# A block-sort attention with an FFT mixer: Sinkhorn on 128 partitions, K and Q of batch 0 ahead of V, variances on ScalarE, add and clamp in one instruction

## The chip, the cores and the metric

The kernel runs on one core of a Trainium2 chip. The time is the device time of one execution in microseconds; the median of three runs before the change is 257.31 us. TensorE is called PE below (PEld are its weight loads), VectorE DVE, ScalarE ACT, GpSimd POOL and SyncE SP.

## The reference

Two stages follow one another: an attention in which the blocks of K and V are first mixed by a matrix P that Sinkhorn's iteration makes, and a Fourier mixer with a feed-forward network. Shortened:

```python
# q, k, v: (4 batches, 8 heads, 768 positions, 64)   sort_net: (4, 8, 8, 8)
P = sort_net
for _ in range(5):
    P = np.exp(P - P.max(-1, keepdims=True))
    P = P / P.sum(-1, keepdims=True)              # rows
    P = P / P.sum(-2, keepdims=True)              # columns
k_s = einsum('bhij,bhjcd->bhicd', P, k in 8 blocks of 96 positions)
v_s = einsum('bhij,bhjcd->bhicd', P, v in 8 blocks of 96 positions)
attn = softmax(q_block @ k_s_block.T / 8)         # in each block, 96 x 96
x = (attn @ v_s) with the heads side by side      # (4, 768, 512)

u = x + real(fft(fft(x, axis=1), axis=2))
un = (u - mean(u)) / sqrt(var(u) + 1e-6)          # over the last axis
out = u + relu(un @ w_ch1) @ w_ch2                # 512 -> 2048 -> 512
```

## The kernel before, in words

The whole work is one list of operations (`P.add`), each with a function that issues its instructions and with the buffers it reads and writes. The order on each engine is not found by the planner: the table `ORDER` gives for each of the five engines the numbers of its operations, and `schedule` only merges the five lists, gives out the pool buffers and works out planned times. These times serve one purpose in the program that is issued: in planned gaps of PE, `spins` puts dummy products (L1973) that read `pack` and write an unused bank, until batch 0's first Fourier results are planned to be done. An instruction waits on the chip only for the semaphores of its data and its buffer.

`tmpk` and `hk` are keys of the buffer `hr`, which holds the feed-forward activations late in the program and, at the start, V of batches 0 and 1 (`hr_72`) and the small tiles of Sinkhorn (`hr_73`).

The work by stages:

- Loads. SP issues the small ones (`pw` from `sort_net`, the constants `pack`, and rows), POOL the large ones: the two halves of V of batches 0 and 1 (`load_v`, 1.5 MB of fp32 each), then the first halves of K and Q of batch 0, then POOL's own memsets, then the second halves of K and Q.
- Sinkhorn (L761 to L776). The 32 matrices (4 batches by 8 heads) stand on 32 partitions, 64 numbers each. Five rounds, each one exponential on ACT and six small DVE instructions. PE then transposes the result, DVE forms `zhi`, `ztm` and `zlo` (L789 to L795), PE spreads `zhi` over partitions, and DVE makes from it `bdk`, the block matrix for K (L805, two halves of the heads), and, in `bdv_make` (L985), the block matrices `bdv16` and `bdv32` for V. ACT keeps a copy, `tkh` (L814), for the later batches.
- V of batches 0 and 1. `v_path` sums V over the positions of a block on PE (psm, L873), copies V in eight parts to `vcx` in the order that the mixing needs (L855 and the `vcp` operations, on ACT and DVE), and `v_mean` and `v_mix` (L945) multiply by `bdv16`; the result goes to `vsf` (L855).
- Attention of a batch, four pairs of heads: `kqt` mixes K (L1140, and L1170 in batch 0) and transposes Q (L1205), `scores` makes the scores (L1236) and ACT their exponentials (L1245), `av` multiplies with V (L1275) and DVE divides into `rt` (L1292).
- Fourier mixer: `dft1` (L1349 and others) along positions, `dft2` (L1427 to L1496) along channels. `dft2` runs for six tiles of 128 positions in each batch. DVE adds x and the transform (L1453 for the first three tiles), then takes the variance with `bn_stats` and `bn_aggr` (L1494, L1496), except for the three tiles of batch 0's first half (`split`), where the sum comes with the addition and DVE scales it (L1483) and ACT takes the squares (L1488).
- Feed-forward. Batches 0 and 1 use `ff1` (L1558) and `mlp` (L1615). Batches 2 and 3 (`SEVEN`) use `ff1_seven` and `ff2_chunk`, a scheme with seven products for eight. There DVE adds a bank and a copy of another (`add`, L1702) and then clamps at zero (`relu`, L1708), in 48 tiles of 128 x 384.

## Time and profile before

| | |
|---|---|
| runs before, us | 257.59, 256.82, 257.31; median 257.31 |
| span of the profiled execution, us | 254.8 (the page lists no time of this execution beside the span) |
| PE busy | 245.2 us, 96% of the span, 2996 products |
| DVE busy | 234.2 us, 92%, 597 instructions |
| ACT busy | 165.3 us, 65%, 376 instructions |
| POOL busy | 57.5 us, 23%, 88 instructions |
| read from and written to memory | 29.07 MB, 6.29 MB; 139 GB/s over the span |
| chain that ended last, by engine | PE 71%, issue 9%, DVE 9%, ACT 8%, POOL 2% |

The profile is of one execution and counts from its first instruction; the span ends with its last. "Busy" is the time in which an engine carried out instructions, its dummy products among them. The chain that ended last is followed back from the last instruction, at each step to what released it. In the prediction's rows a timeline row gives start, length, engine, line, operation, and in brackets the idle time before it with what ended it.

### The profile page before, as it was taken

To read this page: it belongs to the slowest core of one execution; us is meant where nothing else is said; L and a number is where in the kernel's file an instruction comes from. 1 tells how busy PE (TensorE), PEld (TensorE's weight loads), DVE (VectorE), ACT (ScalarE), POOL (GpSimd) and SP (SyncE) were. 2 spreads that over 40 slices of the span, in tenths; PEclk is the share of its full clock that TensorE was granted. 3 is DMA by queue.
4 is the path that set the end of the run, shared out by engine and by line. 5 is a ranking of instruction groups with operands and counts; after the bars stand their busy time and mean duration, and the time that the engine had idled before them with its cause. 6 is when DMAs were issued, how large, how long until landed. Compare 5 with 4: busy or idle time off the path is not lost.

```text
span 254.8 us, 7461 instructions
## 1 busy us (share of the span) xinstructions
PE 245.2 (96%) x2996; PEld 167.0 (66%) x2996; DVE 234.2 (92%) x597; ACT 165.3 (65%) x376; POOL 57.5 (23%) x88
## 2 busy tenths in 40 slices
PE   4999999999999999999999999999999999999992
PEld 1347875566566676644667757888657887567882
DVE  4799998999999989978999998999999999999993
ACT  2599998999968879956797377622687323773000
POOL 8974532234400770003100000210100000050013
PEclk9999999999999999999999999999999999999998
DMA  6999999999942699524132002530202400220025
GB/s 134 202 215 300 210 217 214 208 211 187 150 49 75 86 193 120 64 43 136 44 38 44 1 8 46 98 125 35 82 3 41 84 3 0 85 88 37 3 82 207
DMA packets 42809, 26.54 MB, mean 104 GB/s; under 512 B 30234, under 2 KB 39208, under 8 KB 42772
## 3 DMA queue, kind: packets, MB, share of 16 engines
q0 software_dynamic: 23664, 18.35, 42.9%
q1 hardware_dynamic: 19110, 7.71, 15.0%
q8 instruction: 23, 0.38, 0.6%
q14 instruction: 12, 0.10, 0.1%
HBM read 29.07 MB, written 6.29 MB: 139 GB/s over the span
## 4 chain that ended last, share of the span: by engine, by line
PE 71%; issue 9%; DVE 9%; ACT 8%; POOL 2%; DMA 1%; POOLq 0%; DVEq 0%
PE bank L1558 15%; PE bank L1794 14%; PE bank L1694 12%; PE bank L1615 9%; PE bank L1275 4%; PE bank L1440 3%; PE bank L945 2%; PE bank L1236 2%; ACT vcx L855 2%; PE bank L1349 2%; POOL out_dram L1593 2%; DVE rt L1292 1%; PE bank L1444 1%; PE bank L1047 1%; PE bank L1140 1%
## 5 line engine op out<-in xcount | busy, mean ns | idle before, releaser
L1558 PE MATMUL bank<-ut,w1sb 128*128 128x384 f16 x256 | 48.2, 326 | 0.0
L1714 ACT COPY vsf<-bank 128x384 f32<-128x384 f32 x48 | 21.6, 482 | 24.0 <-PE bank L1694 23.6
L1245 ACT ACTIVATE ex<-bank 96x384 f32<-96x384 f32 x64 | 29.3, 487 | 7.6 <-PE bank L1236 6.2
L1558 PEld LDWEIGHTS <-w1sb 128*128 128x128 f16 x256 | 23.1, 98 | 14.1 <-issue 0.3
L1570 ACT ACTIVATE hr<-bank 128x384 f16<-128x384 f32 x56 | 26.3, 491 | 8.5 <-PE bank L1558 8.5
L1593 POOL DMA_INDIRECT out_dram<-u,rows x9 | 9.4, 1042 | 97.4 <-DVE u L1811 72.5
L1794 PEld LDWEIGHTS <-hr 128*128 128x128 f16 x288 | 28.2, 98 | 4.6
L1702 DVE TENSOR_TENSOR hr<-bank,vsf 128x384 f16<-128x384 f32 x48 | 25.2, 548 | 1.6 <-PE bank L1694 1.0
L1615 PE MATMUL bank<-w2sb,hr 128*128 128x512 f16 x96 | 23.6, 380 | 0.0
L1794 PEld LDWEIGHTS <-vcx 128*128 128x128 f16 x216 | 21.1, 98 | 3.2
L1694 PE MATMUL bank<-ut,w1sb 128*128 128x384 f16 x96 | 20.7, 326 | 0.0
L1794 PE MATMUL bank<-w2sb,hr 128*128 128x256 f16 x144 | 18.7, 272 | 0.0
L1275 PEld LDWEIGHTS <-eb 97*128 97x128 f16 x416 | 15.7, 98 | 3.1 <-issue 0.4
L1794 PE MATMUL bank<-kq,vcx 128*128 128x256 f16 x144 | 17.5, 272 | 0.0
L1694 PEld LDWEIGHTS <-w1sb 128*128 128x128 f16 x128 | 12.5, 98 | 7.5
L612 POOL DMA_DIRECT2D kq<-in_q_dram x18 | 15.4, 866 | 8.8 <-PE bank L1558 4.2
L1292 DVE TENSOR_TENSOR rt<-bank,rz 128x384 f16<-128x384 f32 x32 | 16.9, 547 | 0.2
L1275 PE MATMUL bank<-vsf,eb 97*128 97x65 f16 x416 | 16.9, 193 | 0.0
L855 ACT CAST ks<-bank 128x384 f16<-128x384 f32 x27 | 14.4, 555 | 3.1 <-PE bank L1140 3.0
L1260 ACT ACTIVATE eb<-ex,negone 96x384 f16<-96x384 f32 x26 | 15.9, 616 | 0.1
L855 ACT CAST vsf<-bank 96x512 f16<-96x512 f32 x22 | 14.2, 679 | 1.4 <-PE bank L945 1.4
L1258 DVE TENSOR_SCALAR eb<-ex 96x384 f16<-96x384 f32 x38 | 13.9, 371 | 0.6 <-ACT ex L1245 0.4
(195 smaller groups left out, 535.5 us busy)
## 6 DMA issues: line engine op xcount, KB each, us to landing
w1sb<-in_moe_w_ch_dram POOLq DMA_DIRECT2D x4, 512.0 KB, 18.6
w2sb<-in_moe_w_ch_dram POOLq DMA_DIRECT2D x4, 512.0 KB, 21.5
hr<-in_v_dram POOLq DMA_DIRECT2D x2, 768.0 KB, 8.8
kq<-in_v_dram POOLq DMA_DIRECT2D x2, 768.0 KB, 12.7
kq<-in_k_dram POOLq DMA_DIRECT2D x8, 192.0 KB, 6.5
kq<-in_q_dram POOLq DMA_DIRECT2D x16, 96.0 KB, 6.7
out_dram<-u SPq DMA_DIRECT2D x5, 256.0 KB
kq<-in_k_dram POOLq DMA_DIRECT2D x2, 384.0 KB, 11.7
```

What stands on the lines that cost most here:

```text
L855: (nc.scalar.copy if e == "ACT" else V.tensor_copy)(dst, src)
L1245: nc.scalar.activation(ex.ap[0:96], pss[h2].ap[0:96, 0:384], AF.Exp, scale=SCALE),
L1260: nc.scalar.activation(ed, src, AF.Identity, bias=negone[0:96])
L1275: nc.tensor.matmul(po.ap[:, 65 * T:65 * T + 65], eb.ap[:, e0:e0 + 128], vsf[0:97, vi:vi + 65], start=(n == 0), stop=(n == len(WIN[T]) - 1) ...
L1292: P.add({"DVE": (0.465, 0.56)}, lambda _: V.tensor_tensor(rt.ap[:, :, D * h:D * h + D], po3()[:, :, 0:D], rz.ap[:, :, None].broadcast_to([ ...
L1558: nc.tensor.matmul(ps.ap[:, 0:GT], w1sb[:, c, 128 * fc:128 * fc + 128], ut.ap[:, c, :], start=(c == 0), stop=(c == 3))
L1570: nc.scalar.activation(hr[g][:, fc, :], ps.ap[:, 0:GT], AF.Relu)
L1615: nc.tensor.matmul(ps.ap, hr[g][:, fc, 128 * tt:128 * tt + 128], w2sb[:, fc, :], start=(fc == 0), stop=(fc == 15))
L1694: nc.tensor.matmul(ps.ap[:, 0:GT], lhs[:, c, fi], rhs()[:, c, :], start=(start and c == 0), stop=(c == 1), skip_group_check=True)
L1702: return P.add({"DVE": (0.47, 0.57)}, lambda _: V.tensor_tensor(hr[g][:, fc, :], p.ap[:, 0:GT], o.ap, op=ALU.add), r=r, w=hk(g, fc, fc + 1 ...
L1714: P.add({"ACT": act(GT)}, lambda _: nc.scalar.copy(x.ap, A.ap[:, 0:GT]), r=[A], w=[x], prio=pr_v - 1, tag="pc", after=avs)
L1794: nc.tensor.matmul(ps.ap[:, o:o + 256], lhs()[:, fc], rhs[:, fc], start=(start and fc == 0), stop=(fc == 7), skip_group_check=True)
```

## The change

**Sinkhorn.** The 256 rows of the 32 matrices now stand on 128 partitions in two halves (batches 0 and 1, and 2 and 3), eight numbers on each partition. The first row sum comes with the exponential. A matrix `skc` of constants holds a block matrix of ones, `ones8`: its product with the 128 x 8 tile sums over the eight rows of a matrix and leaves the sum on each of its partitions. The column sums are a DVE accumulation on the same instruction as the multiplication. The first normalization spreads the tile into a block matrix (`spread`) and multiplies it with a selector on PE, which transposes the blocks. Four rounds follow, each with an exponential on ACT, a product on PE and three DVE instructions, for each half. At the end `bdv16` and `bdv32` are made from the tile itself with a mask (L804), `bdk` from one product of `bdv16` of half 0 (L816, L822); `zhi`, `ztm`, `zlo`, `pt` and the function `bdv_make` go.

**Later batches.** `tkh` is no longer a copy on ACT at the start: `make_tk8` makes it by two products from `bdv16` of both halves.

**Loads.** K and Q of batch 0 (first halves) are issued ahead of V's halves; `x0`, `skc` and `x1` ahead of `pack`. The four loads of `w2` keep their places in POOL's order.

**Variances.** `split` holds for all tiles: every variance is taken with the sum that comes with the addition and an ACT square; in tiles 3 to 5 the sum has two parts, added in the scaling.

**Add and clamp.** In `ff1_seven` one custom DVE instruction, `TENSOR_ADD_SAT`, adds and limits to 0 and the largest float.

**Order.** `ORDER` is replaced as a whole, on all engines. Copies of V wait in the program for Sinkhorn operations other than before (`after=`).

```diff
 ORDER = { "PE": (
-        "77 69 78 73 79 91 139 123 125 127 92 97 129 211 141 143 0 103 218 "
+        "0 39 69 43 73 48 78 53 83 88 58 94 97 137 153 141 155 139 157 98 "
...
-    for n, nm in enumerate(("pw", "pack", "vrow", "erow", "rrow",
-                            "rows")):
+    for n, nm in enumerate(("x0", "skc", "x1", "pack", "vrow", "erow",
+                            "rrow", "rows")):
         load_c(nm, -5000.0 + n, "SP")
-    load_v(0, 0, -5000.0)
-    load_v(0, 1, -4999.0)
-    load_qk("k", 0, 0, -4998.0)
-    load_qk("q", 0, 0, -4997.0)
+    load_v(0, 0, -4998.0)
+    load_v(0, 1, -4997.0)
+    load_qk("k", 0, 0, -5000.0)
+    load_qk("q", 0, 0, -4999.0)
...
+        own3 = own[:, :, None].broadcast_to([128, 16, NB])
+        step(d, lambda _: V.tensor_reduce(mx, x, axis=AX.X, op=ALU.max),
+        step(d, lambda _: V.tensor_scalar(z, x, mx, None, op0=ALU.subtract),
+        step({"ACT": (0.3, 0.32)}, lambda _: nc.scalar.activation(
+            E, z, AF.Exp, accum_out=r))
+        step(d, lambda _: V.reciprocal(ri, r))
+        step({"DVE": (0.26, 0.27)}, lambda _: V.scalar_tensor_tensor(
+            spread[t].rearrange("p (g j) -> p g j", j=NB),
+            E[:, None, :].broadcast_to([128, 16, NB]), ri, own3,
+            op0=ALU.mult, op1=ALU.mult), ["skc"])
+        ps = Buf("pf")
+        step(m_, lambda _: nc.tensor.matmul(ps.ap[:, 0:8], spread[t], seli),
+        step(d, lambda _: V.tensor_reduce(
+            cs_, ps.ap[:, 0:8], axis=AX.X, op=ALU.add), [ps])
+        step(d, lambda _: V.reciprocal(ci, cs_))
+        for it in range(4):
+                nc.scalar.activation(E, ps.ap[:, 0:8] if it == 0 else F,
+                                     AF.Exp, scale=ci)
+            step(m_, lambda _, pr=pr: nc.tensor.matmul(
+                pr.ap[:, 0:8], ones8, E), ["skc"], [pr])
+            step(d, lambda _, pr=pr: V.reciprocal(RI, pr.ap[:, 0:8]), [pr])
+            step(d, lambda _: V.scalar_tensor_tensor(
+                F, E, 1.0, RI, op0=ALU.mult, op1=ALU.mult, accum_out=cs_))
+            step(d, lambda _: V.reciprocal(ci, cs_))
+        for n, d_ in enumerate((bdv16[t], bdv32[t])):
+            P.add({"DVE": (0.22, 0.29)}, lambda _, d_=d_:
+                  V.scalar_tensor_tensor(
+                      d_, F[:, None, :].broadcast_to([128, 16, NB]), ci,
+                      own3, op0=ALU.mult, op1=ALU.mult),
...
+        bk.ap[:, 0:64], repk, bdv16[0].rearrange("p g i -> p (g i)")[
+            :, 0:64]), r=[("bdv16", 0), "pack"], w=[bk], tag="psk")
...
-              after=sks[-1:] if b == 0 else [])
+              r=[pt], w=[(qt, 0), (qt, 1)], tag="qtev")
...
-        split = (b, g) == (0, 0)
+        split = True
...
-                return P.add({"DVE": (0.47, 0.57)}, lambda _: V.tensor_tensor(
-                    hr[g][:, fc, :], p.ap[:, 0:GT], o.ap,
-                    op=ALU.add), r=r, w=hk(g, fc, fc + 1), prio=pr_v,
-                    tag="fadd")
-
-            def relu(g, fc):
-                P.add({"DVE": (0.16, 0.24)}, lambda _: V.tensor_scalar(
-                    hr[g][:, fc, :], hr[g][:, fc, :], 0.0, None, op0=ALU.max),
+                return P.add({"DVE": (0.47, 0.57)}, lambda _: V._custom_dve(
+                    TENSOR_ADD_SAT, out=hr[g][:, fc, :], in0=p.ap[:, 0:GT],
+                    in1=o.ap, s0=FMAX, s1=0.0), r=r,
+                    w=hk(g, fc, fc + 1), prio=pr_v, tag="fadd")
```

The changed order, at three places as the instructions stand in the two programs. First the start of ACT, from its table load to batch 0's first exponentials of scores (L1245 before, L1223 after; `vcx` is the copy of V, `ks` and `qt` are K mixed and Q transposed); before:

```order
L711 ACT_TABLE_LOAD
L766 ACTIVATE hr_73<-hr_73 32x64 x5
L855 COPY vcx<-hr_72 128x96x8 x4
L855 CAST ks_77<-bank_64 128x3x8x16
L888 ACTIVATE vb<-vsum 128x128
L855 CAST ks_78<-bank_65 128x3x8x16
L855 CAST ks_78<-bank_61 128x3x8x16
L855 COPY qt_79<-bank_64 128x768
L855 CAST mean_117<-bank_65 128x128
L814 CAST tkh<-bank_62 128x256
L1245 ACTIVATE ex_82<-bank_64 96x384
```

and after:

```order
L777 ACT_TABLE_LOAD
L777 ACTIVATE hr_73<-hr_73 128x8 x2
L792 ACTIVATE hr_73<-bank_61,hr_73 128x8
L792 ACTIVATE hr_73<-bank_62,hr_73 128x8
L792 ACTIVATE hr_73<-hr_73 128x8 x6
L714 ACT_TABLE_LOAD
L863 COPY vcx<-hr_72 128x96x8 x2
L863 CAST ks_78<-bank_63 128x3x8x16
L863 COPY qt_79<-bank_64 128x768
L863 CAST ks_78<-bank_65 128x3x8x16
L863 CAST ks_77<-bank_62 128x3x8x16
L863 COPY vcx<-hr_72 128x96x8
```

Two copies of V instead of four stand ahead of the copies of `ks` and `qt`, the third follows them, the copy to `tkh` is gone, and a second table load stands between Sinkhorn's last exponential and V. Next ACT at its first evacuations of mixed V (`vsf` from a bank of L945 before, of L953 after), with exponentials of scores (`ex`) and other copies about them; before:

```order
L855 CAST vsf<-bank_68 96x64x8
L1245 ACTIVATE ex_82<-bank_63 96x384
L855 CAST vsf<-bank_66 96x64x8
L1245 ACTIVATE ex_84<-bank_63 96x384
L1245 ACTIVATE ex_82<-bank_65 96x384
L855 CAST vsf<-bank_68 96x64x8
L855 COPY rv<-rr 64x255
L855 CAST hi_92<-bank_64 128x257
L855 CAST ks_78<-bank_61 128x3x8x16
L855 COPY rv<-rr 64x256
```

and after:

```order
L863 COPY qt_81<-bank_64 128x768
L863 CAST ks_78<-bank_63 128x3x8x16
L863 COPY un_100<-bank_61 64x4x32
L1223 ACTIVATE ex_83<-bank_62 96x384
L863 CAST vsf<-bank_68 96x64x8
L863 CAST vsf<-bank_63 96x64x8
L863 CAST vsf<-bank_64 96x64x8
L863 CAST vsf<-bank_62 96x64x8
L863 CAST vsf<-bank_65 96x64x8
L863 CAST vsf<-bank_63 96x64x8
L863 CAST ex_83<-bank_64 64x512
L863 COPY qt_79<-bank_61 128x768
```

Three of the copies to `vsf` stood between exponentials of scores; now six follow one another. Last, the end of Sinkhorn on DVE, down to the second copy of V (`bank_61` and `bank_62` in the L805 and L822 rows are the spread matrix for K); before:

```order
L775 RECIPROCAL hr_73<-hr_73 32x8
L776 TENSOR_TENSOR hr_73<-hr_73 32x64
L855 COPY vcx<-hr_72 128x96x8
L789 TENSOR_TENSOR hr_73<-bank_61,pack 64x256
L855 COPY vcx<-hr_72 128x96x8
L805 TENSOR_TENSOR bdk<-bank_62,pack 128x512 x2
L880 TENSOR_REDUCE vsum<-bank_66 128x64
```

and after:

```order
L799 SCALAR_TENSOR_TENSOR hr_73<-hr_73 128x8
L798 RECIPROCAL hr_73<-bank_65 128x8
L799 SCALAR_TENSOR_TENSOR hr_73<-hr_73 128x8
L801 RECIPROCAL hr_73<-hr_73 128x1
L804 SCALAR_TENSOR_TENSOR bdv_0_112<-hr_73 128x128
L863 COPY vcx<-hr_72 128x96x8
L822 TENSOR_TENSOR bdk<-bank_61,pack 128x512
L804 SCALAR_TENSOR_TENSOR bdv_0_111<-hr_73 128x128
L822 TENSOR_TENSOR bdk<-bank_61,pack 128x512
L801 RECIPROCAL hr_73<-hr_73 128x1
L804 SCALAR_TENSOR_TENSOR bdv_1_113<-hr_73 128x128
L863 COPY vcx<-hr_72 128x96x8
```

`bdk` is now made from `bdv16` of half 0 (L804, 128 x 128), with one copy of V ahead of it, instead of from `zhi` (L789); the second half's last reciprocal and `bdv16` come behind `bdk`.

204 lines of the change are left out of this document (81 added, 123 removed), and 199 rows, old and new, of the table ORDER.

## The prediction

> **What bounds the kernel now.** I read the busy time by stage first, then the chain of waits, then the first 30 us instruction by instruction. Busy time by stage (columns: stretch, its length, then busy us and in brackets the instructions of PE, PEld, DVE, ACT and POOL, PE's granted clock, DMA share and GB/s):
>
> ```profile
> 0.00:14.90 14.90, 10.58 (x40) 4.05 (x40) 9.95 (x39) 7.33 (x10) 13.84 (x23) 1.00 0.95 173
> 14.90:43.00 28.10, 27.48 (x540) 19.53 (x540) 27.27 (x73) 26.21 (x61) 11.30 (x18) 1.00 1.17 234
> 43.00:59.00 16.00, 16.00 (x306) 9.83 (x303) 14.30 (x44) 15.30 (x41) 4.54 (x6) 1.00 1.17 210
> 59.00:150.00 91.00, 90.89 (x1350) 57.62 (x1339) 85.51 (x191) 69.67 (x162) 17.55 (x25) 1.00 0.68 83
> 150.00:246.00 96.00, 96.00 (x745) 72.43 (x744) 92.75 (x243) 46.77 (x106) 7.12 (x12) 1.00 0.18 51
> ```
>
> From 59 to 246 us TensorE has work in 186.9 of 187 us. Before that two other engines are full: in 14.9 to 43, VectorE (DVE) 27.2 and ScalarE (ACT) 26.2 of 28.1 us; in 43 to 59, ACT 15.3 and DVE 14.3 of 16. The chain of waits says which of them counts. Its pieces in order of time (start, length, what):
>
> ```profile
> 10.12 5.66 ACT vcx L855 x4
> ...
> 58.53 0.38 ACT hr L1570
> 59.24 1.09 PE bank L1037 x8
> ```
>
> Up to 59 us the chain is mostly ACT and DVE pieces, beginning with the copies of V; from 59.2 us nearly every piece is a matmul. So a microsecond saved on DVE is worth something only ahead of 59 us, and after that the end moves with the time at which TensorE became full. The start, row by row (start, length, engine, line, what; in brackets the idle time before and who ended it):
>
> ```profile
> 1.27 1.32 POOL L612 DMA_DIRECT2D hr<-in_v_dram  x2 [0.82 <-POOLq L1990]
> 2.33 0.21 DVE L761 TENSOR_REDUCE hr<-hr 32x8 f32<-32x64 f32 x1 [1.46 <-DMA hr<-in_sort_net_dram]
> 3.71 4.46 PE L1973 MATMUL bank<-pack 128*128 128x480 f16 x12 [3.71 <-DMA pack<-k_pack]
> 8.66 1.46 PE L873 MATMUL bank<-hr,pack 128*128 128x512 f16 x6 [0.49 <-DMA hr<-in_v_dram]
> 9.95 1.58 PE L1973 MATMUL bank<-pack 128*128 128x480 f16 x7
> 10.03 5.76 ACT L855 COPY vcx<-hr 128x768 f16<-128x768 f16 x4
> 11.39 0.21 DVE L776 TENSOR_TENSOR hr<-hr 32x64 f32<-32x64 f32 x1
> 11.53 0.80 DVE L855 COPY vcx<-hr 128x768 f16<-128x768 f16 x1
> 13.56 1.29 DVE L805 TENSOR_TENSOR bdk<-bank,pack 128x512 f16<-128x512 f32 x2 [0.17 <-PE bank L799]
> 14.93 0.53 PE L1170 MATMUL bank<-bdk,kq 128*64 128x128 f16 x12
> 16.42 0.36 PEld L1205 LDWEIGHTS <-kq 128*64 128x64 f16 x12 [0.21 <-DMA kq<-in_q_dram]
> 18.29 0.49 PE L999 MATMUL bank<-bdv,vb 128*128 128x128 f32 x2
> 19.33 0.41 PE L945 MATMUL bank<-bdv,vcx 128*128 128x64 f16 x8
> ```
> ```profile
> 24.11 0.69 ACT L855 CAST vsf<-bank 96x512 f16<-96x512 f32 x1
> 28.04 0.57 PE L1275 MATMUL bank<-vsf,eb 97*128 97x65 f16 x13
> 250.30 0.42 DVE L1811 TENSOR_TENSOR u<-bank,u 128x256 f32<-128x256 f32 x1 [0.34 <-PE bank L1794]
> ```
>
> Sinkhorn runs from 2.33 to 11.60 us; L789 to L805 turn its result into the block matrix `bdk`; the first product of batch 0 (L1170) starts at 14.93, the first `v_mix` (L945) at 19.33, the first attention product (L1275) at 28.04. TensorE fills its waits with dummy products (L1973). The loads of V behind this (size, us from issue to landing):
>
> ```profile
> hr<-in_v_dram POOLq DMA_DIRECT2D x2, 768.0 KB, 8.8
> ```
>
> The first half of V landed at 8.6 (L873 waited for it) and the second at about 12.2: the mean over both is 8.8, so 17.6 together; the first took 8.6 - 1.27 = 7.3, which leaves 10.3 from the second issue at some 1.9. K and Q of batch 0, of one size, follow in the queue; Q ends L1205's wait at 16.4. So a V half took 3.6 us, K and Q some 2.0 each, and all four were in by 16.2 to 16.4.
>
> **The change part by part.** The unit costs (count, then busy us and mean ns of one):
>
> ```profile
> L770 DVE RECIPROCAL hr<-hr 32x8 f32<-32x8 f32 x5 | 1.0, 191 | 0.2
> L711 ACT ACT_TABLE_LOAD x1 | 1.3, 1283 | 0.7 <-PEq L1990 0.7
> L766 ACT ACTIVATE hr<-hr 32x64 f32<-32x64 f32 x5 | 1.3, 255 | 6.8 <-DVE hr L776 6.0 <-DVE hr L763 0.8
> L789 DVE TENSOR_TENSOR hr<-bank,pack 64x256 f16<-64x256 f32 x1 | 0.4, 403 | 0.0
> L814 ACT CAST tkh<-bank 128x256 f16<-128x256 f32 x1 | 0.4, 381 | 0.0
> L855 ACT CAST ks<-bank 128x384 f16<-128x384 f32 x27 | 14.4, 555 | 3.1 <-PE bank L1140 3.0
> L1494 DVE BATCH_NORM_STATS2 st<-u 128x6 f32<-128x512 f32 x15 | 10.2, 682 | 0.1
> L1496 DVE BATCH_NORM_AGGREGATE mv<-st 128x2 f32<-128x6 f32 x21 | 3.1, 167 | 0.0
> L1483 DVE TENSOR_SCALAR mv<-mv 128x1 f32<-128x1 f32 x3 | 0.5, 153 | 0.1
> L1453 DVE DVE_READ_ACCUMULATOR u<-rt,bank 128x1 f32 x3 | 0.2, 83 | 0.0
> L1488 ACT ACTIVATE ex<-u,mv 128x512 f16<-128x512 f32 x3 | 2.2, 722 | 0.0
> L1488 ACT ACTIVATION_READ_ACCUMULATOR ex<-u,mv 128x1 f32 x3 | 0.6, 186 | 0.0
> L1702 DVE TENSOR_TENSOR hr<-bank,vsf 128x384 f16<-128x384 f32 x48 | 25.2, 548 | 1.6 <-PE bank L1694 1.0 <-ACT vsf L1714 0.3
> L1708 DVE TENSOR_SCALAR hr<-hr 128x384 f16<-128x384 f16 x48 | 10.3, 250 | 0.1
> ```
>
> *Loads.* With K and Q first, V's halves come third and fourth: 16.2 - 3.6 = 12.5 us and 16.2 us, each 3.9 later than now. ACT, which starts copying V at 10.03 (1.44 us a copy), can start at 12.5. K and Q are there by about 9, which nobody needs so early.
>
> *Sinkhorn.* `pack` is now fourth on SP's queue instead of second. From the first small load's landing (2.33) to `pack`'s (3.71) are 1.4 us, an upper bound for one issue; I take 0.45 each, so the dummies start at 3.7 + 0.9 = 4.6, and two of them at 0.4 us stand ahead of the first Sinkhorn product: 5.4. Its operand is ready about 4.5 (2.33, then two maxima and two subtractions, an exponential, reciprocals and the spread tile, nine small steps of about 0.24). Such a product has no row; L999, also fp32 with 128 weight columns, takes 0.49 for 128 columns, so for 8 columns between 0.25 and 0.5; I take 0.4. Sum and reciprocal then cost 2 x 0.19 and two handovers, and `ci` of half 0 stands at 6.2. One round is an exponential (0.26 at most), a product (0.4), three small DVE instructions (0.19), and five gaps of 0.05: 1.48 us. (Today five rounds take 9.27 us with the start, 1.85 each, of which one exponential and six DVE instructions of 0.2 are 1.46: 0.39 for seven gaps.) Four rounds end at 12.1. But the table for TensorE puts half 1's last product and five dummies ahead of half 0's last, which waits for the other half's exponential: +0.9, 13.0. The masked matrix `bdv16`, 0.3 beside the 0.40 of L789, makes it 13.3. Today the same point, `zhi` behind the copy that ends at 12.33, is 12.7. So Sinkhorn saves no time by itself (bounds: 12.4 without the cross wait, 14.9 if the products run as slowly as the dummies do at first).
>
> *To the first product.* On DVE a copy of V (0.80) stands ahead of `bdk`, and its data have been in since 12.5: 13.3 + 0.8 + half of 1.29 = 14.75. On TensorE seven dummies (7 x 0.22) and the six V sums (1.46) stand ahead of the first product: from 12.7 on 1.5 + 1.5, so 15.7 at the latest, 14.9 if the dummies were done earlier. I take 15.0 for the first product, as now.
>
> *From there to attention.* V's second half at 16.2, three plus three V sums around scores that wait for ACT (two copies to 15.4, then four evacuations of `ks` and `qt` at 0.55 to 17.6), reduction 0.7, mean and its masked form about 1.9: the first `v_mix` at about 21.5 instead of 19.33. The table for TensorE puts more of batch 0 ahead of it: all 48 K products of batch 0, 36 Q transposes and 32 score products, where now 24, 24 and 8 are. So the eight `v_mix` follow one another, and ACT takes six of their evacuations in a row: 21.5 + 0.5 + 6 x 0.69 = 26.2 for the first attention product, against 28.04: 1.85 us earlier. That is the term that carries the forecast.
>
> *Variances.* In batch 0's second half three DVE statistics (0.68 + 0.17 each) go and three scalings (0.15) and six accumulator reads (0.08) come: -1.6 us on DVE. ACT gains three squares at 0.72 + 0.19: +2.7. The two engines have 0.7 + 1.7 = 2.4 us free in 43 to 59, and the sum rises by 1.1, so most of it fits; I charge 0.35, between 0 (copies move to DVE in the new tables) and 1.35 (half of 2.7). For the other 18 tiles, after 59 us, DVE loses 18 x 0.85 = 15 us and regains about 5, beside a full TensorE: 0.
>
> *Add and clamp.* 48 clamps (0.25 each) go from batches 2 and 3. The fused instruction has no row; its bounds are the add, 0.55, and add plus clamp, 0.80, and I take 0.55 since it reads the same two fp32 operands. All of it lies beside a full TensorE: 0 either way, since even 0.80 is today's sum. *Tail:* the same last product, addition (250.30) and store: 0. *Second table load on ACT:* the first one, at the very start, ends ahead of the data; the second takes 1.28 us. Its last exponential ends at 11.2 without the cross wait and at about 12.05 with it (13.0 less a product, two DVE steps and gaps), so ACT is ready for V at 12.5 or at 13.3, where V lands at 12.5. Half of such a delay would be lost, since DVE does not share it: 0 to 0.4, and I charge 0.2.
>
> The Trainium skill, "ScalarE: Activation LUTs", What ACT_TABLE_LOAD costs, gives about 1.38 us of drain behind each load, 2.66 in all. By that the copies of V would start 1.4 later, and half of that would be lost: a gain of 0.6 instead of 1.3. No row of the trace can tell: after the only load ACT waited for data.
>
> **Sum.** -1.85 + 0.35 + 0.2 = -1.3 us on a span of 254.8: 253.5. The page lists no time of the profiled execution beside its span; the three runs' median, 257.31, lies 2.5 us above the span, and I keep that: **256.0 us**.
>
> **Rivals.** *VectorE was the hidden bound* (faster still). In 150 to 246 DVE is busy 92.8 of 96 us; if matmuls wait briefly for it, the 22 us or so taken off DVE (15 - 5 for the variances, 12 for the clamps) would show. For: 97%. Against: TensorE's row is 96.00 of 96. A tenth of 22 us recovered gives 253.8.
>
> *Cold TensorE* (no change). In the start the first dummies come every 0.4 us (12 in 4.46 us), after 9.95 every 0.2. Both clocks read 1.00 in the stage rows, so this is not the granted clock. After the change the first dummies are spread between waits, and if the fast pace comes only after some 4 us without a break, the five and the seven dummies in Sinkhorn's end run at 0.4: +1.0 and +1.4 less 0.5 of slack, and `bdk` comes 1.9 later: 257.9. For: 12 dummies in a row needed 4 us. Against: 5 + 7 may be enough. The Trainium skill, "TensorE: Matmul & The Clock Gate", Part 1, states this rule: half rate until about 3.4 us of sustained work; the 4 us of slow dummies agree with it.
>
> *ACT and DVE start too late* (slower). The chain up to 59 us runs on these two, and both stand idle longer: ACT begins at 12.5 instead of 10.03 (+2.5), DVE is free of Sinkhorn at 13.3 instead of 11.6 (+1.7). Work taken from them there: `zhi` and its two companions 1.2, `tkh` 0.4. (4.2 - 1.6) / 2 = +1.3: 258.6. For: both are over 93% busy from 14.9 to 43. Against: the work done first is now what the chain needs first. It decides once the first attention product comes later than 28.0.
>
> **How the numbers follow.** Forecast 0.50, hidden bound 0.17, cold TensorE 0.12, late start 0.21. The runs before spread over 0.77 us, so 0.3% (0.8 us) is about what a measurement tells from no change. Faster: 0.50 + 0.17 = 0.67; same: 0.12, less 0.01 of it; slower: 0.21 + 0.01 = 0.22. Low end: the hidden bound's 253.8 with the cross wait (0.8) and the table's share (0.2) gone, 252.8. High end: the late start, 258.6, and 0.3 for its spread, 258.9.
>
> **What would show it.** Right: V's first copy on ACT between 12.5 and 13.3, first product near 15, first `v_mix` near 21.5, first attention product near 26.2, TensorE full from about 57.5, the fused instruction at 0.55. Wrong: the first attention product after 28, dummies at 0.4 us behind 10 us, or waits of TensorE between 59 and 246 that shrink.

## The result, and the profile after

The changed kernel takes 269.4 us (median of four runs, 268.43 to 269.66) against 257.09 before: a ratio of 1.047, 95% interval 1.045 to 1.050. The forecast was 256.0, with a range up to 258.9. The profiled span is 267.9 us, 13.1 more than before; time less span is 1.8 us in this execution (269.66), not the 2.5 that the forecast carried over. Medians below leave out runs more than 1.5% above the fastest of their kernel: two of four with the other form of L775 alone, one of four in the fourth corner. Busy time by stage, with the edges and columns of the prediction's first table:

```profile
0.00:14.90 14.90, 3.28 (x12) 1.98 (x12) 10.29 (x13) 2.31 (x7) 13.84 (x24) 1.00 0.91 171
14.90:43.00 28.10, 27.05 (x349) 17.73 (x350) 23.27 (x81) 22.26 (x44) 8.17 (x14) 1.00 0.86 163
43.00:59.00 16.00, 15.42 (x332) 10.39 (x330) 15.24 (x46) 14.92 (x36) 4.07 (x6) 1.00 1.06 211
59.00:150.00 91.00, 90.22 (x1448) 57.19 (x1446) 83.39 (x218) 68.70 (x167) 20.93 (x29) 1.00 0.90 105
150.00:246.00 96.00, 96.00 (x736) 70.11 (x733) 88.05 (x220) 54.88 (x133) 6.64 (x12) 1.00 0.16 46
```

In the first 14.9 us ACT has done 2.3 us of work instead of 7.3 and TensorE 12 products instead of 40; from 59 to 246 us TensorE has work in 186.2 of 187 us, where it was 186.9. The loss lies in the start. Its rows (start, length, engine, line, what, idle time before):

```profile
3.13 0.16 DVE L773 TENSOR_REDUCE hr<-hr 128x1 f32<-128x8 f32 x1 [0.49 <-DMA hr<-in_sort_net_dram]
3.21 8.24 DVE L775 TENSOR_SCALAR hr<-hr 128x8 f32<-128x8 f32 x2
4.07 5.84 POOL L700 MEMSET eb<- 96x1672 f16 x4
6.90 0.98 PE L1953 MATMUL bank<-pack 128*128 128x480 f16 x2 [6.90 <-DMA pack<-k_pack]
10.57 0.45 POOL L712 MEMSET negone<- 128x1 f32 x1
11.47 0.21 ACT L777 ACTIVATE hr<-hr 128x8 f32<-128x8 f32 x1 [9.45 <-DVE hr L775]
```
```profile
19.88 1.28 ACT L714 ACT_TABLE_LOAD   x1
21.18 2.90 ACT L863 COPY vcx<-hr 128x768 f16<-128x768 f16 x2
21.25 2.68 PE L1953 MATMUL bank<-pack 128*128 128x480 f16 x7
22.09 0.35 DVE L804 SCALAR_TENSOR_TENSOR bdv<-hr 128x128 f16<-128x128 f32 x1
25.19 0.53 PE L1149 MATMUL bank<-bdk,kq 128*64 128x128 f16 x12
32.53 0.41 PE L953 MATMUL bank<-bdv,vcx 128*128 128x64 f16 x8
```
```profile
38.65 0.97 PE L1253 MATMUL bank<-vsf,eb 97*128 97x65 f16 x26
```

Both maxima are there at 3.3 us, and the two subtractions behind them (L775, eight numbers on each partition) end at 11.45: ACT gets its first exponential after 9.45 us of waiting. In those 8.2 us POOL issues the loads of V and then carries out its memsets (4.07 to 11.02) without a pause. No semaphore shows this wait: the row counts it as the instruction's own time, and 8.24 of DVE's 10.29 busy us in the first stage are this standing still. So an instruction here does not wait for the semaphores of its data and its buffer alone. Everything behind is late by that and more: `bdv16` of half 0 ends at 22.44 (13.3 forecast), the first product of K comes at 25.19 (15.0), the first `v_mix` at 32.53 (21.5), the first attention product at 38.65 (26.2; 28.04 before).

### The profile page after: what moved, and what is told of

Same layout as the page of the kernel before. It is cut to its first block, busy times and chain, and to the rows that moved or that the text cites. A ratio compares the mean times of both kernels' runs of the same rounds, so it can differ in the third digit from the quotient of the medians.

```text
span 267.9 us, 7506 instructions
## 1 busy us (share of the span) xinstructions
PE 247.8 (92%) x3006; PEld 171.2 (64%) x3006; DVE 235.5 (88%) x607; ACT 165.0 (62%) x388; POOL 57.3 (21%) x88
## 4 chain that ended last, share of the span: by engine, by line
PE 73%; issue 10%; DVE 6%; ACT 5%; POOL 2%; DMA 1%; POOLq 0%; SPq 0%; DVEq 0%; ACTq 0%
PE bank L1547 16%; PE bank L1775 13%; PE bank L1683 9%; PE bank L1604 8%; PE bank L1253 4%; DVE hr L775 3%; PE bank L1418 3%; PE bank L1327 3%; PE bank L1214 2%; PE bank L1953 2%; POOL out_dram L1582 2%; ACT ex L1223 2%; PE bank L953 2%; PE bank L881 1%; PE bank L1422 1%
## 5 line engine op out<-in xcount | busy, mean ns | idle before, releaser
L1547 PEld LDWEIGHTS <-w1sb 128*128 128x128 f16 x256 | 23.4, 98 | 14.9 <-issue 0.4
L1582 POOL DMA_INDIRECT out_dram<-u,rows x9 | 10.2, 1137 | 105.7 <-DVE u L1792 73.5
L1223 ACT ACTIVATE ex<-bank 96x384 f32<-96x384 f32 x64 | 29.0, 489 | 3.7 <-PE bank L1214 2.4
L1691 DVE CUSTOM_DVE_ANT_0 hr<-bank,vsf 128x384 f16<-128x384 f32 x48 | 25.1, 552 | 5.4 <-PE bank L1683 4.6
L1559 ACT ACTIVATE hr<-bank 128x384 f16<-128x384 f32 x44 | 20.8, 488 | 7.3 <-PE bank L1547 7.2
L1775 PEld LDWEIGHTS <-vcx 128*128 128x128 f16 x216 | 21.1, 98 | 3.3
L863 ACT CAST vsf<-bank 96x512 f16<-96x512 f32 x21 | 13.6, 684 | 9.8 <-PE bank L953 9.7
L1775 PE MATMUL bank<-w2sb,hr 128*128 128x256 f16 x144 | 18.0, 273 | 0.0
L1253 PE MATMUL bank<-vsf,eb 97*128 97x65 f16 x416 | 17.5, 193 | 0.5 <-issue 0.4
L1236 DVE TENSOR_SCALAR eb<-ex 96x384 f16<-96x384 f32 x48 | 16.5, 357 | 0.9 <-ACT ex L1223 0.9
L1683 PEld LDWEIGHTS <-w1sb 128*128 128x128 f16 x128 | 12.5, 98 | 7.4
L1953 PE MATMUL bank<-pack 128*128 128x480 f16 x26 | 10.4, 503 | 6.9 <-DMA pack<-k_pack 6.9
L1683 PE MATMUL bank<-qt,kq 128*128 128x384 f16 x64 | 14.8, 326 | 0.0
## 6 DMA issues: line engine op xcount, KB each, us to landing
w2sb<-in_moe_w_ch_dram POOLq DMA_DIRECT2D x4, 512.0 KB, 21.9
out_dram<-u SPq DMA_DIRECT2D x5, 256.0 KB
```

The costliest lines, as they stand in the source:

```text
L1223: nc.scalar.activation(ex.ap[0:96], pss[h2].ap[0:96, 0:384], AF.Exp, scale=SCALE),
L1236: V.tensor_scalar(ed, src, -1.0, None, op0=ALU.add)
L1253: nc.tensor.matmul(po.ap[:, 65 * T:65 * T + 65], eb.ap[:, e0:e0 + 128], vsf[0:97, vi:vi + 65], start=(n == 0), stop=(n == len(WIN[T]) - 1) ...
L1547: nc.tensor.matmul(ps.ap[:, 0:GT], w1sb[:, c, 128 * fc:128 * fc + 128], ut.ap[:, c, :], start=(c == 0), stop=(c == 3))
L1559: nc.scalar.activation(hr[g][:, fc, :], ps.ap[:, 0:GT], AF.Relu)
L1683: nc.tensor.matmul(ps.ap[:, 0:GT], lhs[:, c, fi], rhs()[:, c, :], start=(start and c == 0), stop=(c == 1), skip_group_check=True)
```

## The experiments

### Is it the form of one instruction, against POOL?

Three kernels. In the first the subtraction takes another form; in the second the old kernel gets one small instruction of the suspected form; in the third POOL's long memsets go to DVE, ahead of its first data.

```diff
-        step(d, lambda _: V.tensor_scalar(z, x, mx, None, op0=ALU.subtract),
+        step(d, lambda _: V.tensor_tensor(
+            z, x, mx.broadcast_to([128, NB]), op=ALU.subtract),
```

> The changed kernel, with only the subtraction of the maximum (L775) in another form: a TENSOR_TENSOR with the maximum broadcast over the eight numbers, the form that the kernel before uses at L763, instead of a TENSOR_SCALAR with the maximum as scalar. Theory POOL: the two TENSOR_SCALARs (8.2 us each, both done at 11.45) stand still because POOL carries out memsets from 4.07 to 11.0 us. Then the subtractions take about 0.2 us each, the first exponential starts near 3.6 instead of 11.47, everything up to the first product of batch 0 moves up by some 7.9 us, and the time is about 261.5 us (between 260.5 and 262.5). Theory DATA: they wait for a load or for ACT; then the form changes nothing: 269.4 us. About 4.4 us over the kernel before stay in either case, from something else.

```diff
 # the kernel before
                 V.tensor_tensor(pw, pw, rmax ..., op=ALU.subtract)
+                V.tensor_scalar(rs, rmax, rmax[:, 0:1], None, op0=ALU.subtract)
```

> The kernel before with one more DVE instruction: behind the subtraction of L763 a TENSOR_SCALAR from SBUF to SBUF, 32 x 8 fp32, whose result nothing reads. Theory POOL: it stands until POOL's memsets end at 11.0 us, so Sinkhorn ends some 7.5 to 8 us later and the time is 263 to 266 us. Theory DATA, or a small instruction's own price: +0.2 us, 257.3 us.

```diff
-        P.add({"POOL": (1.5, 1.6)}, lambda _, n=n: nc.gpsimd.memset(
+        P.add({"DVE": (0.45, 0.5)}, lambda _, n=n: nc.vector.memset(
             eb4[0:96, n, :], 0.0), w=[("ebz", n)], ...)
```

> The changed kernel with the four memsets of eb (5.84 us of POOL's 7) on DVE at the very start, where DVE waits for its first data until 2.48; L775 keeps its form. Theory POOL: the memsets that stay on POOL then run from 4.07 to about 5.3, and the subtractions end there, or at the end of the DMA issues behind them if these count too (about 6), instead of at 11.45: 263 to 264.5 us. Theory DATA: 269.4 us. The four memsets on DVE themselves: 0.5 us each, ended before 2.5, nothing.

Timeline rows of the three, in this order:

```profile
3.07 0.28 DVE L775 TENSOR_TENSOR hr<-hr 128x8 f32<-128x8 f32 x2
7.02 0.98 PE L1954 MATMUL bank<-pack 128*128 128x480 f16 x2 [7.02 <-DMA pack<-k_pack]
8.27 0.17 DVE L788 TENSOR_REDUCE hr<-bank 128x1 f32<-128x8 f32 x1 [3.44 <-PE bank L786]
20.51 0.53 PE L1150 MATMUL bank<-bdk,kq 128*64 128x128 f16 x12
```
```profile
2.69 8.28 DVE L767 TENSOR_SCALAR hr<-hr 32x8 f32<-32x8 f32 x1
10.85 0.16 POOL L705 MEMSET pmt<- 128x6 f16 x1
```
```profile
4.43 1.29 DVE L776 TENSOR_SCALAR hr<-hr 128x8 f32<-128x8 f32 x2
4.80 0.49 POOL L709 MEMSET pmt<- 128x6 f16 x1
```

Theory POOL holds in all three. With the other form both subtractions take 0.28 us in the same place. One TENSOR_SCALAR whose result nobody reads, put into the kernel before, takes 8.28 us there, until POOL's last memset ends (11.01), and costs 10.5 us (267.24 against 256.78; ratio 1.040, 1.038 to 1.042). With four memsets off POOL the pair takes 1.29 us and ends at 5.72, 0.43 after the last memset, as in the changed kernel (11.45 and 11.02). The Trainium skill, "SBUF — State Buffer", SBUF: two separate sides, states a rule of this kind: DVE and POOL share a pair of ports; of a DVE operation in a two-port mode and a POOL operation the one that starts first holds the pair for the whole instruction, and a DVE operation with two SBUF inputs is shut out only by a POOL operation that reads SBUF. The three runs agree with it in which form waits (a memset reads nothing); beyond it, the wait here goes on through a whole row of POOL instructions, nine memsets and the DMA issues ahead of them. Whether the issues alone would hold DVE stays open: in the second kernel the instruction begun at 2.69 was not done when the memsets began at 4.04, and POOL had only issued loads until then; but in the kernel before, copies of V on DVE (11.53 and 12.59) took their 0.80 us while POOL issued loads.

The size was wrong in the first: 264.4 us (263.0 to 268.1 over all four runs) instead of 261.5, a span of 264.1. The rows show why. Sinkhorn's first product, ready since 4.8, stands behind two dummies which wait for `pack` until 7.02, and DVE waits 3.44 us with it. In the changed kernel this wait (6.90) lay hidden behind the stall. The third came out as expected (264.5), though its four memsets took 0.85 us each on DVE, not 0.5, so that the first maximum starts only at 4.29.

The second cost more than the 263 to 266 us that I expected. The stall is some 8 of its 10.5 us; Sinkhorn's result reaches TensorE 7.95 us later than in the kernel before (19.61 against 11.66), but the first product of K comes 10.41 later (25.34 against 14.93). TensorE had waited 7.6 us for that result, and its granted clock reads one half, until 25.1 us (columns as in the table of stages; the kernel before reads 1.00 in this stretch):

```profile
14.90:23.00 8.10, 3.39 (x10) 1.24 (x11) 5.33 (x21) 5.43 (x6) 2.67 (x4) 0.50 1.18 297
```

The six V sums take 2.95 us at that clock instead of 1.63.

### Dummies and `pack`

```diff
-                if o.start < max(x.end for x in goal):
+                if o.start < max(x.end for x in goal) and o.tag not in ("sink", "psk"):
                     for _ in range(spins(t, o.start - 0.05)):
```

> As the kernel with the other form of L775, and besides it without the dummy products that are placed between Sinkhorn's products on TensorE (17 of 26; those in front of the V sums and later stay). It asks what of the 4.4 us over the kernel before is due to slow TensorE. If dummies at 0.4 us in front of Sinkhorn's products delay them (five before the last product of half 0, seven before the block matrix's product): 0.5 to 2 us faster than that kernel, about 260. If they keep TensorE warm and the products behind them take half the time: slower by 0.5 to 2 us, 262 to 263.5.

The same edit with the change's own form of the subtraction:

> The changed kernel with its TENSOR_SCALAR at L775 and without the 17 dummy products in Sinkhorn: the fourth corner beside 269.4 (both as changed), 266.9 (other form, with dummies) and 262.1 (other form, no dummies). Theory SHADOW: the wait for pack (6.9 us) lies behind the stall (11.45), so taking the dummies away here brings only what the five and the seven late dummies cost, 1 to 1.7 us, and not the 4.8 that it brought with the other form: 267.5 to 268.5. Rival, both causes add up: 264.6.

And the dummies kept, `pack` second on SP (the SP row of `ORDER` begins with x0, pack, x1, skc):

> The kernel with the other form of L775, with all its dummy products, and with pack issued second on SP (x0, pack, x1, skc) instead of fourth. In the kernel with the other form alone, pack landed at 7.02 us, and the first dummies and behind them the first product of Sinkhorn waited for it: DVE idle from 4.8 to 8.3. Theory PACK: with pack landing near 4, that product starts near 5 instead of 7.8 and the time falls by 2.5 to 3 us from that kernel's, to about 263.5 to 264. Rival: what holds the first product is skc, which now lands last, or the traffic of K and Q: then no gain, 266 to 267 us.

Timeline rows of the first of these three, without the dummies:

```profile
4.76 1.02 PE L786 MATMUL bank<-hr 128*128 128x8 f32 x4 [4.76 <-DVE hr L781]
6.18 1.02 PE L797 MATMUL bank<-hr 128*128 128x8 f32 x4 [0.39 <-ACT hr L793]
7.95 1.18 PE L797 MATMUL bank<-hr 128*128 128x8 f32 x4 [0.75 <-ACT hr L793]
9.71 1.18 PE L797 MATMUL bank<-hr 128*128 128x8 f32 x4 [0.59 <-ACT hr L793]
13.60 2.92 ACT L864 COPY vcx<-hr 128x768 f16<-128x768 f16 x2 [0.27 <-DMA hr<-in_v_dram]
14.23 2.74 PE L882 MATMUL bank<-hr,pack 128*128 128x512 f16 x6
16.90 0.85 PE L1150 MATMUL bank<-bdk,kq 128*64 128x128 f16 x12
```
```profile
27.14 3.59 ACT L864 CAST vsf<-bank 96x512 f16<-96x512 f32 x6
31.31 0.97 PE L1254 MATMUL bank<-vsf,eb 97*128 97x65 f16 x26
```

And with `pack` second:

```profile
3.66 1.78 PE L1954 MATMUL bank<-pack 128*128 128x480 f16 x4 [3.66 <-DMA pack<-k_pack]
6.78 0.61 DVE L781 SCALAR_TENSOR_TENSOR hr<-hr 128x128 f32<-128x128 f32 x2 [1.89 <-DMA hr<-k_skc]
```

Without the dummies the first product comes at 4.76 and the time falls to 262.1 us, 2.3 less than with the other form alone. The two runs behind that one's median lie 2.8 us apart, so the size is rough; the first product of K comes 3.6 earlier (16.90 against 20.51). Both are more than the 0.5 to 2 us expected, because the wait for `pack` was not in it. Not all of the gain arrives: the six V sums ahead of that product take 2.74 us (14.23) instead of 1.46 with dummies, and the twelve products 0.85 instead of 0.53.

The traces say why. Their records of the granted clock begin at 7.5 us in the kernel before, at 23.5 in the changed kernel, at 19.1 with the other form and at 19.6 without dummies. Ahead of its first record the stage rows count the clock as 1.00 for want of one, but products there keep the pace that they have at a recorded 0.50 (V sums 0.46 us each here, 0.49 in the second kernel above), and the fast pace begins with the record. That TensorE has half its clock until then is inferred from the pace; that it is slow for 12 to 16 us longer than before, with the dummies and without them, is what the rows show.

With the stall in place the same edit brings nothing: 270.6 (269.0 to 272.4), above the 267.5 to 268.5 expected. The first product of K comes 0.4 us earlier (24.75 against 25.19), since the V sums ahead of it take 2.74 us there too. In spans the four corners read 267.9 and 267.3 with the stall, 264.1 and 260.4 without. SHADOW holds in its mechanism: two causes in a row on one path, and the second pays only once the first is gone. With `pack` second it lands at 3.66, but then `skc` lands at 6.78 and DVE waits for that: 265.2 instead of 263.5 to 264, one small load late instead of another.

### The loads

Four trials to give the new start its data. V ahead of K and Q on POOL, then also `skc` second on SP:

> The kernel with the other form of L775 and without dummies in Sinkhorn (262.1 us), with the two halves of V ahead of K and Q on POOL's queue again. There the first copies of V on ACT started at 13.60, when V had landed, and the sums of V's first half stood in front of the first product of batch 0, which came at 16.90 with its block matrix ready at 15.5 and at 16.3. Theory LOADS: with V in at 8.6 and 12.2 and K and Q in by 14.3 and 16.2, the V sums are done before the block matrix is ready, the first product comes near 15.8, the V halves' copies are no longer waited for, and the time is 260 to 261. Rival: ACT is at its second table load until 13.3 and the later order holds the rest; then 261.8 to 262.4. Other side: Q, now in at 16.2, is waited for: 262.5 to 263.

> The kernel with the other form of L775 and without dummies in Sinkhorn (262.1 us), with V ahead of K and Q on POOL and SP's loads as x0, skc, x1, pack. With V first and skc third, skc landed behind V's first half, at 8.5, and Sinkhorn began 4.2 us later (266.1 us). Theory QUEUE: a small load that SP issues before about 1.3 us gets through ahead of the large ones; with skc second (1.20) it lands near 3.7, Sinkhorn runs as in the kernel at 262.1, V is in at 8.5 and 12.6, pack at 12.8, and the sums of V are done before the block matrix is ready; the first product comes at 15.6 to 16: 260 to 261. Rival, Q (17.3) and pack late are waited for: 262 to 263. Rival, skc late all the same: 265 to 267.

Then `sort_net` in one load, and the six V sums behind the first products of K; and this without the dummies that the plan put ahead of those:

```diff
-        x0=(xs[:, 0], sort_net[0:2].rearrange("b h i j -> (b h i) j"), 4096),
+        x0=(xs, sort_net.rearrange("(t b) h i j -> (b h i) t j", t=2), 8192),
 # PE row of ORDER
-        ... 94 97 137 153 141 155 139 157 98 ...
+        ... 94 137 153 141 155 139 157 97 98 ...
```

> The kernel with the other form of L775 and without dummies in Sinkhorn (262.1 us), with four things moved at the start: sort_net as one load instead of two, skc second on SP, V ahead of K and Q on POOL, and the six sums of V's first half behind the first products of K instead of ahead of them. Theory QUEUE: SP's first two loads get through ahead of V (land by 4), Sinkhorn begins at about 4 as there, V is in at 8.6 and 12.6, and the first product comes when the block matrix is ready, at 15 to 15.5 instead of 16.9: 259.5 to 261. Rival, the start is not what is left: 262.

> The kernel with one load of sort_net, skc second, V first and V's sums behind the first K products (263.7 us), without the 15 dummies that the planner put ahead of the first products of K and Q in it. There the block matrix's halves were ready at 14.8 and 15.6, and the first K product, behind eight dummies, came at 16.84. Theory DUMMIES: it comes at 15.0 to 15.7, and the time is 260.5 to 262. Rival, TensorE is colder then and the products behind take twice as long: 262.5 to 264.

The rows that decided, one or two of each kernel in this order:

```profile
3.18 0.16 DVE L773 TENSOR_REDUCE hr<-hr 128x1 f32<-128x8 f32 x1 [0.64 <-DMA hr<-in_sort_net_dram]
8.60 0.61 DVE L781 SCALAR_TENSOR_TENSOR hr<-hr 128x128 f32<-128x128 f32 x2 [4.46 <-DMA hr<-k_skc]
```
```profile
9.12 0.23 DVE L773 TENSOR_REDUCE hr<-hr 128x1 f32<-128x8 f32 x2 [9.12 <-DMA hr<-in_sort_net_dram]
```
```profile
13.53 3.38 PE L1958 MATMUL bank<-pack 128*128 128x480 f16 x8
16.84 0.54 PE L1153 MATMUL bank<-bdk,kq 128*64 128x128 f16 x12
```
```profile
15.44 0.85 PE L1153 MATMUL bank<-bdk,kq 128*64 128x128 f16 x12 [1.46 <-DMA kq<-in_k_dram]
17.42 0.85 PE L1188 MATMUL bank<-pack,kq 128*64 128x128 f16 x12 [1.12 <-DMA kq<-in_q_dram]
```

None gained on 262.1: 266.1, 267.4, 263.7 and 263.5 us. As ratios to the kernel before, measured beside each, these are 1.037, 1.040, 1.025 and 1.022, against 1.022 for the kernel of 262.1: the last is as fast as that one, not slower. A small load that SP issues third (1.66 us) waits for the large ones that POOL has issued meanwhile: `skc` until 8.60 behind V, or x1 until 9.12 when `skc` took its place; x0 and x1 in the first two places are through by 3.2. With K and Q first `skc` in third place came by 4.3. So the change's order of loads is the one that its three small loads bear, and my theory QUEUE was right on the mechanism and wrong each time on the sum. With the loads in order, eight dummies (13.53, 0.42 each) held the first product until 16.84; without them K (15.44) and Q (17.42) were waited for, and the twelve products of K took 0.85 us instead of 0.54. The time lies where the rival, a colder TensorE, had put it (262.5 to 264): the clock's first record stands at 21.9 us there, at 16.9 with the dummies.

### The late parts

Variances back on DVE, in the kernel of 262.1 us; and, in the kernel before, add and clamp fused alone.

```diff
+        real = (b, g) == (0, 0)
-            if split:
+            if real:
                 sq = Buf("ex")
```

> The kernel with the other form of L775 and without dummies in Sinkhorn (262.1 us), with the variances of the 21 tiles back on DVE (BN statistics) and off ACT, each at the place in DVE's order behind where its scaling stood. Theory COVERED: all but batch 0's three tiles lie beside a full TensorE; the time stays at 262.1 within 0.6. Theory ACT: the squares on ACT are part of what is left over the kernel before; then 260.5 to 261.5. Theory DVE: the change's variances save DVE time that counts; then 263 to 265.

> The kernel before, with only the 48 additions and clamps of batches 2 and 3 in the one custom instruction and the 48 clamps (0.25 us each) gone; order otherwise as before. Theory COVERED: TensorE is full there, so the time stays at 256.8 within 0.4 although DVE loses some 10 us of work. Theory HIDDEN BOUND: TensorE waits briefly for DVE in 150 to 246; then 254 to 256.

Groups of DVE by form (count, busy us and mean ns, idle before) in the kernel before, then in the kernel of 262.1 us; and TensorE and the rest between 59 and 246 us, in that kernel and in the one with the variances on DVE:

```profile
L1258 DVE TENSOR_SCALAR eb<-ex 96x384 f16<-96x384 f32 x38 | 13.9, 371 | 0.6 <-ACT ex L1245 0.4
L1567 DVE TENSOR_SCALAR hr<-bank 128x384 f16<-128x384 f32 x8 | 4.3, 545 | 0.0
L855 DVE CAST ks<-bank 128x384 f16<-128x384 f32 x5 | 2.9, 581 | 0.7 <-PE bank L1140 0.7
```
```profile
L1692 DVE CUSTOM_DVE_ANT_0 hr<-bank,vsf 128x384 f16<-128x384 f32 x48 | 25.1, 552 | 5.4 <-PE bank L1684 4.6 <-ACT vsf L1699 0.3
L1237 DVE TENSOR_SCALAR eb<-ex 96x384 f16<-96x384 f32 x48 | 16.7, 360 | 1.0 <-ACT ex L1224 0.9
L1557 DVE TENSOR_SCALAR hr<-bank 128x384 f16<-128x384 f32 x20 | 11.0, 548 | 1.0 <-PE bank L1548 0.6
L864 DVE CAST ks<-bank 128x384 f16<-128x384 f32 x13 | 7.1, 571 | 1.7 <-PE bank L1150 1.6 <-PE bank L1120 0.2
```
```profile
59.00:246.00 187.00, 186.78 (x2127) 129.23 (x2125) 172.31 (x422) 118.46 (x285) 25.33 (x38) 1.00 0.45 67
```
```profile
59.00:246.00 187.00, 179.11 (x2066) 119.92 (x2059) 173.94 (x399) 105.55 (x243) 23.81 (x37) 1.00 0.47 65
```

The fused instruction takes 0.552 us, as the plain addition (0.548). Alone it changes nothing: 256.8 (ratio 1.000, 0.998 to 1.003), COVERED. The variances were the miss: 274.9 us, 12.5 more (each against the kernel before measured beside it), far outside every theory. TensorE, busy for 186.8 of 187 us without that edit, works 179.1 with it: 7.7 us of waiting stand in these stages alone. In the profiled run a granted clock of 0.5 from 43.5 to 46.9 us adds to the loss. The groups show why they can arise: the changed order has given DVE other work in exchange, 48 evacuations of `eb` instead of 38, 20 ReLUs of the feed-forward (L1557) instead of 8, 13 casts of `ks` and its like instead of 5, together 34.8 us against 21.1. So 13.7 us of what variances and clamps had left free are used again, and the variances on DVE stand on top of that. In this order the variance on ACT is not idle relief; the order is built on it. What the variances would do in the old order, without that exchange, was not tried.

### What is left: start, order or tail

Three kernels take the old order, the old Sinkhorn and the old loads up to 16, 20 and 26 us of the plan, and the changed order, variances and fused instruction from there on.

> The kernel before up to about 16 us of its plan (Sinkhorn on 32 partitions, loads, block matrices, first products in the old order), and from there on the changed kernel: its order on every engine, variances on ACT, add and clamp fused. Theory START: all that the change loses lies in its start; then this is at or below the kernel before, 254.5 to 257.5 us, since the changed order brings the attention of batch 0 forward. Theory REST: the changed order after the start costs what the kernel at 262.1 still lacked, 4 to 5 us: 260 to 262.

> As the kernel with the old start up to 16 us, with the old order kept up to about 20 us of the plan (the first mixings of V among it). Theory START: 255 to 257.5. Theory REST: between 257.5 and 261. What it adds: if it is nearer to the kernel before than the one with 16 us, the order between 16 and 20 us, where the changed kernel puts batch 0's K, Q and scores ahead of V, is what costs.

> As these two, with the old order kept up to about 26 us of the plan. From here on only the late parts of the change and its late order are in it, where TensorE is full or nearly so. Theory COVERED: 256.5 to 257.5, as the kernel before. Rival, the late order leaves TensorE waiting or has a longer tail (1.6 us): 258 to 259.

Two look at the end of the program. One puts its last 68 operations into the old order, in the kernel of 262.1:

> The kernel with the other form of L775 and without dummies in Sinkhorn (262.1 us), with the last 68 operations of the program (second layer of batch 3, its sums, additions and stores) in the order of the kernel before on each engine. Theory TAIL: there TensorE's last product ended 1.6 us nearer to the end of the span (254.8 - 250.3 before, 260.4 - 254.3 in this kernel), because more of the output is left to write then; with the old order the time falls by 1.2 to 1.8 us, to 260.3 to 260.9. Rival, the last store's landing alone sets the rest whatever the order: 262.1.

The other, in the kernel with the old start up to 20 us, only moves the middle tile's last two products, two additions and its store to the end (`ORDER` of PE then ends with `1520 1531`, as before):

> The kernel with the old order up to 20 us and the changed rest (258.8 us), with the end of the program in another order: the last two products of the middle tile, their two additions and its store go behind everything else, as in the kernel before. In its profile TensorE was done at 249.8, as early as before, but the span went on for 6.3 us after that instead of 4.6, since three tiles' last parts were still to be written. Theory TAIL: 1 to 1.5 us faster, 257.3 to 257.8, the kernel before within 0.3%. Rival, TensorE then waits ahead of its last products for as long (as where all 68 last operations were put in the old order): 258.5 to 259.

The last store through POOL and the last addition: changed kernel, old start up to 20 us, and the latter with the tail moved:

```profile
261.68 0.75 DVE L1792 TENSOR_TENSOR u<-bank,u 128x256 f32<-128x256 f32 x2
262.04 0.96 POOL L1582 DMA_INDIRECT out_dram<-u,rows  x1 [1.44 <-DVE u L1792]
```
```profile
249.58 0.92 DVE L1823 TENSOR_TENSOR u<-bank,u 128x256 f32<-128x256 f32 x2
249.94 0.96 POOL L1606 DMA_INDIRECT out_dram<-u,rows  x1 [1.08 <-DVE u L1823]
```
```profile
249.24 0.96 POOL L1606 DMA_INDIRECT out_dram<-u,rows  x1 [0.19 <-DVE u L1823]
250.75 0.43 DVE L1823 TENSOR_TENSOR u<-bank,u 128x256 f32<-128x256 f32 x1 [0.59 <-PE bank L1806]
```

With the old start up to 16, 20 and 26 us: 261.0, 258.8 and 261.3 us, against 257.55 for the kernel before, measured beside them. START, which put them at about the kernel before or below it, fails in the first two, whose times lie in REST's ranges; the third is outside both of its ranges. So with the old start and 20 us of the old order, 1.3 us of the 12.3 are left (ratio 1.006, 1.004 to 1.008); the cut at 26 shows that the two orders do not join equally well everywhere, so these differences hold for the joint as well. In the profile of the kernel cut at 20 the last addition ends at 250.5, as early as before (250.72), but the span goes on to 256.0 instead of 254.8. With the tail moved POOL's last store is issued at 249.24, ahead of the last products, and the span ends 4.2 us behind the last addition (251.2 to 255.4) instead of 5.5; the time is 258.3 (ratio 1.002, 1.0005 to 1.004). TAIL is right in the profile; the medians differ by 0.5 us where 1 to 1.5 were expected, and the two intervals overlap. The 68 operations in the old order gave no gain (263.0, from 261.3 to 264.8): inconclusive at that spread. No version beat the kernel before.

## Why the prediction was wrong

**The bound** was read rightly: what counts is when TensorE becomes full, and after 59 us little but the tail adds. The first attention product is 10.6 us later than before, the last addition 11.7 (262.43 against 250.72), and the tail adds 1.4.

**Sinkhorn** is the step that failed. "Nine small steps of about 0.24" put the first product's operand at 4.5 us; two of the nine took 8.2 us together. No row of the kernel before had a TENSOR_SCALAR with SBUF operands while POOL's memsets ran, so its price had to be bounded from both sides, and was instead taken from its neighbours. The row of POOL's memsets was not read at all. Besides, a round took 1.77 us, not 1.48 (products at 6.18, 7.95, 9.71 in the kernel without dummies): two products for two halves occupy TensorE for 1.0 to 1.2, so 0.5 to 0.6 each, the upper end of "between 0.25 and 0.5" and above. Sinkhorn by itself was not far off: without stall and dummies `bdv16` stands at 14.15, where I had 13.3, within my bounds of 12.4 to 14.9.

**`pack`** was to land at 4.6; it landed at 6.9. The two further small loads ahead of it cost more than the 0.45 us that I took for each issue: in the kernel without the stall `skc` ended a wait at 4.35, with K's load under way beside it. **V** ended ACT's first wait for it at 13.6 in the kernel without the stall, where I had 12.5.

**The gain at batch 0's attention**, -1.85 us, the term that carried the forecast, never came: even without stall and dummies that product starts at 31.31, later than 28.04. Two terms of it were too small. The first `v_mix`, for which I had 21.5, comes at 25.19 there: TensorE is busy nearly all the way from the V sums at 14.23 on, until 19.6 at the slow pace. And from it to the first attention product I counted 0.5 us and six evacuations, 4.7 in all, where 6.1 pass: ACT begins the six (27.14) only 1.95 us after that `v_mix`, behind copies of `qt`, `ks` and `un` and an exponential that the sum left out.

**Variances and clamp**: 0 for the clamp is what the fused instruction alone shows. The 0.35 for batch 0 was not measured by itself. "Beside a full TensorE: 0" left out that the order hands DVE other work for it. **Tail**: 0 forecast, 1.4 measured; the last product is not the same one.

**The second table load** costs its 1.28 us and no more: it starts at 19.88 and the copy of V behind it at 21.18. The further 1.38 us of drain that the Trainium skill, "ScalarE: Activation LUTs", What ACT_TABLE_LOAD costs, gives do not show here, neither behind the load nor ahead of it (the last exponential ends at 19.87).

**The rivals.** Hidden DVE bound: refuted by the fused instruction alone (256.8). Cold TensorE: its condition held. The dummies still come every 0.4 us at 23 us, and the seven in front of the block matrix's product stand until 23.8, though its operand is there at 22.44. "So this is not the granted clock" was a wrong reading: the stage rows' 1.00 stands for a missing record, and the records begin at 7.5 us before the change and at 23.5 after it. What this costs by itself was not measured; taking the dummies away doesn't remove it. Late start: the right sign and the right place, and past its point (28.0) in every kernel with the new start; at 262.1 without stall and dummies up to 5.3 us are its share, not 1.3. With the old start until 20 us of the plan 4.0 of these 5.3 go (each against the kernel before measured beside it). In the kernel of 262.1 the first product of K is 2.0 us later than before the change, the first `v_mix` 5.9 and the first attention product 3.3. How they split between Sinkhorn's length, the cold TensorE, V's later landing and the order behind it is not settled.

## What to carry to other kernels

An instruction's price in the trace holds for what ran beside it there: before moving to a new form on DVE, look at what POOL does in those microseconds, and use a form that is known to run beside it. Such a wait has no semaphore and counts as busy time, so a single row that is much longer than its size needs is the sign to look for. When a stall is removed, the next wait behind it becomes visible, so cost the path to its end, and try two suspected causes both singly and together. A change that frees an engine and an order that fills it again cannot be judged apart.

## What was not expected of the hardware

A DVE instruction of eight numbers per partition stood for 8.2 us beside POOL's memsets, in two programs. SP's third small load, issued 0.4 us behind POOL's first large one, ended a wait at 8.60, the second, issued 0.46 us earlier, one at 3.18. Dummy products with short pauses between them kept the 0.4 us pace until 23 us, where the stage rows read a granted clock of 1.00; the first record of that clock stands at 23.5. After 7.6 us without work TensorE ran at a recorded 0.50 for 5.5 us of work (19.6 to 25.1) before the full clock came back.
